# Attention in 64x64 tiles of TensorE, and router logits summed per head from the product that turns the outputs back

## The chip, the cores and the metric

The kernel runs on one NeuronCore of a Trainium2 chip. Its engines work side by side: TensorE (PE in the rows; PEld are its weight loads) multiplies matrices into PSUM, VectorE (DVE) and ScalarE (ACT) work element by element, GpSimd (POOL) does small work and indirect DMA, SyncE (SP) issues DMA. The metric is the time on the device in microseconds (us), the median of several runs; lower is better. The profile is of one execution.

## The reference

Block-sparse attention for 4 batches of 8 heads with 768 positions of 64 numbers, and then a mixture of 8 experts, of which a router with cosine similarity picks one for each of the 3072 tokens.

```python
# attention; mask[i, j] is set where the blocks of 32 positions of i and j are neighbours, one of
# them is the first or the last, or j's block is one of three drawn for i's
scores = np.where(mask, scale * np.matmul(q, k.transpose(0, 1, 3, 2)), -1000000000.0)
attn = np.exp(scores - np.max(scores, axis=-1, keepdims=True))
attn = attn / (np.sum(attn, axis=-1, keepdims=True) + 1e-09)
x = np.matmul(attn, v)                       # then (B, H, S, D) -> (B*S, H*D): 3072 x 512
...
xn = x / (np.linalg.norm(x, axis=-1, keepdims=True) + 1e-6)
en = expert_emb / (np.linalg.norm(expert_emb, axis=-1, keepdims=True) + 1e-6)
logits = xn @ en.T / tau
expert_idx = np.argmax(logits, axis=1)       # probs: the softmax of the logits
gate_w = probs[np.arange(N), expert_idx]
for e in range(E):
    mask = expert_idx == e
    out[mask] = gate_w[mask, None] * (np.maximum(x[mask] @ w1[e], 0.0) @ w2[e])
```

## The kernel before

Everything is float32 but the mask, which is bfloat16. There are two parts, one behind the other.

**Attention** (`attention_fast`). Work goes by pairs of heads, 16 of them, and in each pair by two halves of 384 queries. A half has six units, one for each 128 keys, so there are 192 units. `load_pair` brings a pair's keys, queries and values two pairs ahead. `turn_fast` turns keys and queries with TensorE, in four parts per pair (three 128x128 transposes each, copied out by VectorE for keys and by ScalarE for queries). `score_fast` makes a unit's scores for both heads: a mask product (24 rows of block numbers, line 272) opens each head's sum in PSUM, the product of keys and queries (64 rows, 128 columns of weights, line 275) closes it, and ScalarE takes the exponent (line 278) into SBUF, tile `e`. `attend_fast` multiplies `e` by the values: 128 rows and 64 columns of weights for each head (line 295), summed over the six units in PSUM tile `av`; VectorE sums `e` itself over the units into `esum` (lines 291 and 293). Behind the sixth unit ScalarE copies `av` to `at` (line 299). A float32 product of this kernel is two passes of TensorE, each with its weight load; so line 275 has 768 passes for 384 products.

`settle` ends a half, one unit later than its last: three transposes turn `at` back (line 313), six products with a column of ones make the sums over keys from `esum` (line 317, twelve passes of one column), and VectorE writes the outputs divided by these sums into `x` (line 323), one tile for a batch.

`route` follows each batch (four times): ScalarE squares `x` in six pieces (line 353) for the norms, POOL takes the root (line 354), TensorE transposes `x` in 24 blocks (line 363), VectorE copies them out (line 365), and 24 products in 48 passes of 8 columns (line 368) make the logits `lg` against the experts' normed vectors `en`. VectorE then finds the largest logit's place as a one-hot tile `oh` (line 385). Two small products (`rk`, lines 401 and 402) give each token its rank within its expert, of which the second waits for POOL's running counts `seen` (line 399).

`dispatch` then sorts the tokens into tiles of 128 of one expert (VectorE, and 24 products `slot_ps`).

**Experts.** For each of 27 such tiles weights and tokens are fetched by DMA, tokens transposed (`xg_ps`), multiplied by w1 (line 510) and w2 (line 518) and scattered to the output.

What sets the order: each engine has one queue in program order. The loop of `attention_fast` (line 545) names score products one unit ahead of the attention products, the turns in between, and settle and route behind the attention product of a half's second unit; the framework places the instructions of `route` among those of the following units by its own estimates. PSUM tiles come from pools: scores and router transposes from `big` (two buffers of two banks), `av` from `acc` (two buffers of one bank), everything small from `small` (two of one bank).

## Time and profile before

| | us |
|---|---|
| median of three runs | 1002.25 |
| lowest and highest run | 997.63, 1003.86 |
| the profiled execution, its run | 999.39 |
| the profiled execution, its span | 997.6 |
| mean granted TensorE clock | 0.947 |

Times in rows count from the span's start. A row of the timeline has a start, a length, the engine, the line, the operation, the tiles written and read with their shapes, the count of merged instructions and, in brackets, how long the engine sat idle before it and what ended that. A TensorE instruction's length contains its way through the array, so lengths of neighbours overlap, and the distance of starts is what one costs. The granted clock is a share of 2.4 GHz: 1.00 and 0.50 are the two levels.

### The profile page before, as it was taken

Reading aid. Unit: us, or ns where it says so; the run is one execution under the profiler, and the core shown is the slowest. Engines: PE = TensorE matmul, PEld = TensorE weight load, DVE = VectorE, ACT = ScalarE, POOL = GpSimd, SP = SyncE. Lnnn points to the kernel's source line nnn. Section 1 sums busy time; section 2 is a strip of 40 time slices with the busy share of each in tenths; the row PEclk is TensorE's granted clock in tenths of the full one; section 3 lists DMA queues with packets and bytes.
Section 4 is the critical chain, followed back from the end, with each engine's and each line's share of the span. In section 5 each row is a group of like instructions: output and inputs, shape, how many; then the busy total and the mean of one; then the engine's idle time right before and its main releaser. Section 6 shows DMA issues by size and latency. Waiting matters only on the chain.

```text
span 997.6 us, 12554 instructions
## 1 busy us (share of the span) xinstructions
PE 942.3 (94%) x5230; PEld 542.6 (54%) x5230; DVE 298.0 (30%) x513; ACT 218.0 (22%) x340; POOL 73.1 (7%) x105
## 2 busy tenths in 40 slices
PE   5999999999999999999998489999999999999984
PEld 2344354344454434634446466766776776776662
DVE  2444443444434444334444511111111111111110
ACT  2434432433423444233342000000000000000000
POOL 1000000000010000100001100110110111111010
PEclk9999996999979999789996589999999999999997
DMA  7111112111221111020001299989889998998872
GB/s 174 30 34 49 48 32 80 48 44 37 48 79 33 48 49 32 17 79 1 1 1 42 102 400 407 401 311 342 306 314 329 311 326 316 330 321 314 289 280 77
DMA packets 105243, 161.69 MB, mean 162 GB/s; under 512 B 52620, under 2 KB 56716, under 8 KB 104662
## 3 DMA queue, kind: packets, MB, share of 16 engines
q1 hardware_dynamic: 100694, 146.84, 43.3%
q0 software_dynamic: 4480, 13.91, 3.5%
q8 instruction: 45, 0.74, 0.3%
q14 instruction: 24, 0.20, 0.1%
HBM read 148.14 MB, written 13.38 MB: 162 GB/s over the span
## 4 chain that ended last, share of the span: by engine, by line
PE 89%; issue 5%; DVE 2%; DMA 1%; SPq 1%; ACT 0%; POOL 0%; POOLq 0%; ACTq 0%
PE sc L275 18%; PE hp L510 18%; PE yp L518 17%; PE av L295 16%; PE sc L272 5%; PE back L317 4%; PE turn L257 3%; PE lg L368 3%; PE back L313 2%; PE xg_ps L501 1%; PE slot_ps L462 1%; PE xt_ps L363 1%; DMA out_dram<-y,slot 1%; SPq L173 1%; DVE xt L365 0%
## 5 line engine op out<-in xcount | busy, mean ns | idle before, releaser
L278 ACT ACTIVATE e<-sc 128x768 f32<-128x768 f32 x192 | 155.6, 810 | 287.3 <-PE sc L275 287.3
L510 PEld LDWEIGHTS hp<-xgt,w 128*128 128x128 f32 x1728 | 199.5, 192 | 25.4 <-issue 11.0
L510 PE MATMUL hp<-xgt,w 128*128 128x128 f32 x1728 | 204.2, 277 | 9.1 <-ACT h L513 4.9
L275 PE MATMUL sc<-qt,kt 64*128 64x384 f32 x768 | 192.4, 556 | 0.0
L518 PE MATMUL yp<-w,h 128*128 128x512 f32 x432 | 189.9, 592 | 0.0
L295 PE MATMUL av<-e,vld 128*64 128x384 f32 x768 | 173.1, 523 | 0.0
L293 DVE TENSOR_TENSOR esum<-esum,e 128x768 f32<-128x768 f32 x128 | 122.3, 956 | 105.9 <-ACT e L278 105.9
L518 PEld LDWEIGHTS yp<-w,h 128*128 128x128 f32 x432 | 80.0, 190 | 90.4 <-issue 90.4
L513 ACT ACTIVATE h<-hp 128x512 f32<-128x512 f32 x27 | 16.1, 597 | 412.7 <-PE hp L510 383.7
L295 PEld LDWEIGHTS av<-e,vld 128*64 128x64 f32 x768 | 39.2, 137 | 81.9 <-issue 63.4
L275 PEld LDWEIGHTS sc<-qt,kt 64*128 64x128 f32 x768 | 62.6, 191 | 35.9 <-issue 35.8
L272 PEld LDWEIGHTS <-kmask 24*128 24x128 bf16 x384 | 18.2, 91 | 102.3 <-issue 101.8
L520 DVE TENSOR_SCALAR y<-yp,xg 128x512 f32<-128x512 f32 x27 | 20.3, 750 | 158.6 <-PE yp L518 158.6
L514 DVE TENSOR_SCALAR h<-hp 128x512 f32<-128x512 f32 x27 | 18.7, 691 | 160.9 <-PE hp L510 160.9
L272 PE MATMUL sc<-qmask,kmask 24*128 24x384 bf16 x384 | 66.5, 340 | 0.0
L291 DVE TENSOR_TENSOR esum<-e 128x768 f32<-128x768 f32 x32 | 30.7, 958 | 110.6 <-ACT e L278 110.6
L521 POOL DMA_INDIRECT out_dram<-y,slot x27 | 27.5, 1017 | 352.9 <-DVE y L520 338.5
L317 PEld LDWEIGHTS back<-ones,esum 128*128 128x128 f32 x384 | 45.4, 192 | 0.0
L317 PE MATMUL back<-ones,esum 128*128 128x1 f32 x384 | 44.7, 243 | 0.0
L354 POOL TENSOR_TENSOR nrm<-nrm,half 128x6 f32<-128x6 f32 x4 | 5.3, 1330 | 485.3 <-ACT sq L353 485.3
L368 PEld LDWEIGHTS lg<-en,xt 128*128 128x128 f32 x192 | 29.4, 242 | 6.3 <-DVE xt L365 4.6
L486 POOL DMA_INDIRECT xg<-x_dram,slot x29 | 29.9, 1032 | 29.2 <-DVE slot L464 20.6
(124 smaller groups left out, 392.8 us busy)
## 6 DMA issues: line engine op xcount, KB each, us to landing
w<-in_moe_w_dram SPq DMA_DIRECT2D x58, 2048.0 KB, 9.4
x_dram<-x SPq DMA_DIRECT2D x4, 1539.0 KB, 6.1
kld<-in_k_dram SPq DMA_DIRECT2D x32, 192.0 KB, 3.0
qld<-in_q_dram SPq DMA_DIRECT2D x32, 192.0 KB, 3.2
vld<-in_v_dram SPq DMA_DIRECT2D x16, 384.0 KB, 3.2
xg<-x_dram,slot POOLq DMA_INDIRECT x29, 7.4
out_dram<-y,slot POOLq DMA_INDIRECT x27, 7.4
x_dram<-zero SPq DMA_DIRECT2D x1, 2.0 KB
```

The source lines that it names most:

```text
L257: nc.tensor.transpose(ps[:, c * P:(c + 1) * P], src[:, lo + c].rearrange("p h d -> p (h d)"), k.ident)
L272: nc.tensor.matmul(ps[:, h, 0:HALF], lhsT=k.kmask[32 * h:32 * h + NB, keys], rhs=k.qmask[32 * h:32 * h + NB, queries], start=True, stop=False)
L275: nc.tensor.matmul(ps[:, h, 0:HALF], lhsT=kt[D * h:D * (h + 1), keys], rhs=qt[D * h:D * (h + 1), queries], start=False, stop=True)
L278: nc.scalar.activation(e, ps[:, :, 0:HALF], ACT.Exp)
L291: nc.vector.tensor_tensor(out=k.esum, in0=k.first, in1=e, op=ALU.add)
L293: nc.vector.tensor_tensor(out=k.esum, in0=k.esum, in1=e, op=ALU.add)
L295: nc.tensor.matmul(k.av[D * h:D * (h + 1), 0:HALF], lhsT=v[:, h, kc, :], rhs=e[:, h, :], start=(kc == 0), stop=(kc == NC - 1))
L317: nc.tensor.matmul(ps[:, i:i + 1], lhsT=esum[:, h, t * P:(t + 1) * P], rhs=k.ones[:, 0:1], start=True, stop=True)
L368: nc.tensor.matmul(lg[:, c, :], lhsT=xt[:, (c - c2) * ND + d, :], rhs=k.en[:, d, :], start=(d == 0), stop=(d == ND - 1))
L486: nc.gpsimd.indirect_dma_start(out=x[:, :], out_offset=None, in_=k.x_dram[:, :], in_offset=bass.IndirectOffsetOnAxis(ap=k.slot[:, t:t + 1] ...
L510: nc.tensor.matmul(hp[:, f, :], lhsT=w1[:, d, f * P:(f + 1) * P], rhs=xt[:, d, :], start=(d == 0), stop=(d == ND - 1))
L518: nc.tensor.matmul(yp, lhsT=h[:, f, :], rhs=w2[:, f, :], start=(f == 0), stop=(f == NF - 1))
```

## The change

It has six parts.

1. Masks, scores and attention products are cut into quarters: 64 rows (a head, or half of a unit's keys) by 64 columns. The mask's two tiles are widened from 24 to 64 rows of zeros for this. A unit has four mask products, four score products and four attention products where it had two of each; the sizes of `sc`, `e` and `esum` stay.
2. The attention products of the two halves of keys are summed apart: `av` has two banks, `acc` has one buffer in place of two, and behind the sixth unit ScalarE copies one bank (`part`) and VectorE adds the other to it (`at`).
3. `settle` turns back with a real product: its right side `back` has, for each of the two heads, a unit matrix of 64 columns and the 8 columns of `en` that belong to that head, 144 columns together. So partial logits per head come out beside the outputs; VectorE divides these too and keeps them in `part` for the batch.
4. `route` adds up the eight heads' partial logits on VectorE (`reduce_sum`); its transposes, their copies and its logit products are left out. They remain for the exact path, which runs only where a sum over keys is out of bounds.
5. The loop names scores two units ahead, settle and route first in a unit, then the attention product, a turn (at other units than before), and the scores.
6. Setup fills the mask tiles and `back`.

```diff
         for h in range(2):
-            nc.vector.tensor_copy(out=k.kmask[32 * h:32 * h + NB, :], in_=krow)
-            nc.scalar.copy(out=k.qmask[32 * h:32 * h + NB, :], in_=qr[0:NB, 0:S])
+            nc.vector.tensor_copy(out=k.kmask[D * h:D * h + NB, :], in_=krow)
+            nc.scalar.copy(out=k.qmask[D * h:D * h + NB, :], in_=qr[0:NB, 0:S])
...
+    k.back = k.const.tile([P, NPAIR, 2, D + E], F32, name="back")
+    nc.gpsimd.memset(k.back, 0.0)
+    for h in range(2):
+        rows = slice(D * h, D * (h + 1))
+        nc.vector.tensor_copy(out=k.back[rows, :, h, 0:D],
+                              in_=k.ident[rows, rows].unsqueeze(1).broadcast_to([D, NPAIR, D]))
+        nc.vector.tensor_copy(out=k.back[rows, :, h, D:D + E], in_=k.en[rows])
...
-    keys, queries = slice(kc * P, (kc + 1) * P), slice(qh * HALF, (qh + 1) * HALF)
-    for h in range(2):
-        nc.tensor.matmul(ps[:, h, 0:HALF], lhsT=k.kmask[32 * h:32 * h + NB, keys],
-                         rhs=k.qmask[32 * h:32 * h + NB, queries], start=True, stop=False)
-    for h in range(2):
-        nc.tensor.matmul(ps[:, h, 0:HALF], lhsT=kt[D * h:D * (h + 1), keys], rhs=qt[D * h:D * (h + 1), queries],
-                         start=False, stop=True)
+    queries = slice(qh * HALF, (qh + 1) * HALF)
+    quarters = [(h, r, slice(kc * P + D * r, kc * P + D * (r + 1))) for r in range(2) for h in range(2)]
+    for rows, cols, first in ((k.kmask, k.qmask, True), (kt, qt, False)):
+        for h, r, keys in quarters:
+            nc.tensor.matmul(ps[D * r:D * (r + 1), h, 0:HALF], lhsT=rows[D * h:D * (h + 1), keys],
+                             rhs=cols[D * h:D * (h + 1), queries], start=first, stop=not first)
...
-        k.av = k.acc.tile([P, 512], F32, name="av", tag="av")
+        k.av = k.acc.tile([P, 2, 512], F32, name="av", tag="av")
...
-    for h in range(2):
-        nc.tensor.matmul(k.av[D * h:D * (h + 1), 0:HALF], lhsT=v[:, h, kc, :], rhs=e[:, h, :],
-                         start=(kc == 0), stop=(kc == NC - 1))
+    for r in range(2):
+        for h in range(2):
+            nc.tensor.matmul(k.av[D * h:D * (h + 1), r, 0:HALF], lhsT=v[D * r:D * (r + 1), h, kc, :],
+                             rhs=e[D * r:D * (r + 1), h, :], start=(kc == 0), stop=(kc == NC - 1))
     if kc == NC - 1:
+        part = k.sp.tile([P, HALF], F32, name="part", tag="part")
+        nc.scalar.copy(out=part, in_=k.av[:, 1, 0:HALF])
         at = k.sp.tile([P, HALF], F32, name="at", tag="at")
-        nc.scalar.copy(out=at, in_=k.av[:, 0:HALF])
+        nc.vector.tensor_tensor(out=at, in0=k.av[:, 0, 0:HALF], in1=part, op=ALU.add)
...
     for t in range(NQ):
-        nc.tensor.transpose(ps[:, t * P:(t + 1) * P], at[:, t * P:(t + 1) * P], k.ident)
+        nc.tensor.matmul(ps[:, t * 2 * W:(t + 1) * 2 * W], lhsT=at[:, t * P:(t + 1) * P],
+                         rhs=k.back[:, j].rearrange("p h w -> p (h w)"), start=True, stop=True)
...
+    nc.vector.tensor_tensor(out=k.part[b][:, chunks, 2 * j:2 * j + 2, :], in0=rows[:, :, :, D:W],
+                            in1=inv.unsqueeze(3).broadcast_to([P, NQ, 2, E]), op=ALU.mult)
...
+    lg = logits(k, x) if k.exact else l
+    if not k.exact:
+        nc.vector.reduce_sum(out=l, in_=k.part[b].rearrange("p c h e -> p c e h"), axis=AX.X)
...
-    n.big, n.acc = pool("big_f", 2, space=PSUM), pool("acc", 2, space=PSUM)
+    n.big, n.acc = pool("big_f", 2, space=PSUM), pool("acc", 1, space=PSUM)
...
     score_fast(n, 0)
+    score_fast(n, 1)
     for u in range(units):
         g = u // per
         if u % per == 0 and g + 2 < pairs:
             load_pair(n, g + 2)
-        if u + 1 < units:
-            score_fast(n, u + 1)
-        if u % per in (2, 4, 8, 10) and g + 1 < pairs:
-            turn_fast(n, g + 1, (2, 4, 8, 10).index(u % per))
-        attend_fast(n, u)
         if u % NC == 1 and u > NC:
             settle(n, u // NC - 1)
             if (u - 1) % (per * NPAIR) == 0:
                 route(n, (u - 1) // (per * NPAIR) - 1)
+        attend_fast(n, u)
+        if u % per in (2, 3, 5, 8) and g + 1 < pairs:
+            turn_fast(n, g + 1, (2, 3, 5, 8).index(u % per))
+        if u + 2 < units:
+            score_fast(n, u + 2)
```

Three places of the order show how it stands in the queues. In these rows `x4` counts products that follow each other, and the shape is that of what is written.

TensorE before, around a settle: the end of one unit's scores, its attention products, the settle (`back`), and the next unit with a turn.

```order
L275 MATMUL sc<-qt,kt 128x384 x2
L295 MATMUL av<-e,vld 64x384 x2
L313 MATMUL back<-ident,at 128x128 x3
L317 MATMUL back<-ones,esum 128x1 x6
L272 LDWEIGHTS kmask
L272 MATMUL sc<-qmask,kmask 128x384
L272 LDWEIGHTS kmask
L272 MATMUL sc<-qmask,kmask 128x384
L275 MATMUL sc<-qt,kt 128x384 x2
L257 MATMUL turn<-ident,qld 128x128 x3
L295 MATMUL av<-e,vld 64x384 x2
```

TensorE with the change, around a settle: from the end of a unit's scores to the next unit's first score product.

```order
L283 MATMUL sc<-qt,kt 64x384 x4
L327 MATMUL back<-back,at 128x144 x3
L332 MATMUL back<-ones,esum 128x1 x6
L304 MATMUL av<-e,vld 64x384 x4
L283 LDWEIGHTS kmask
L283 MATMUL sc<-qmask,kmask 64x384
L283 LDWEIGHTS kmask
L283 MATMUL sc<-qmask,kmask 64x384
L283 LDWEIGHTS kmask
L283 MATMUL sc<-qmask,kmask 64x384
L283 LDWEIGHTS kmask
L283 MATMUL sc<-qmask,kmask 64x384
```

Products are twice as many and half as tall, the settle stands ahead of the attention products, and its transposes have become products of 144 columns.

TensorE before, at the first router pass, behind the settle of the batch's last half:

```order
L313 MATMUL back<-ident,at 128x128 x3
L317 MATMUL back<-ones,esum 128x1 x6
L363 MATMUL xt_ps<-ident,x 128x128 x15
L295 MATMUL av<-e,vld 64x384
L368 MATMUL lg<-en,xt 128x8 x8
L295 MATMUL av<-e,vld 64x384
L363 MATMUL xt_ps<-ident,x 128x128 x9
L368 MATMUL lg<-en,xt 128x8 x8
```

TensorE with the change, at the first router pass; ahead of these rows and behind the settle stand the attention products of two units and the scores of one.

```order
L283 MATMUL sc<-qt,kt 64x384 x4
L304 MATMUL av<-e,vld 64x384
L425 MATMUL rk<-oh,before 128x48
L266 MATMUL turn<-ident,kld 128x128 x2
L426 MATMUL rk<-seen,ones 128x48
L266 MATMUL turn<-ident,kld 128x128
L304 MATMUL av<-e,vld 64x384 x3
L283 LDWEIGHTS kmask
L283 MATMUL sc<-qmask,kmask 64x384
L266 MATMUL turn<-ident,kld 128x128 x3
```

Transposes and logits are gone; the rank products stand two units behind the settle, in the middle of an attention product's quarters and a turn.

ScalarE with the change, at the first router pass (`e<-sc` are exponents of units, `part<-av` the new copy of an accumulator's bank, `sq` the squares):

```order
L286 ACTIVATE e<-sc 128x768 x3
L308 COPY part<-av 128x384
L286 ACTIVATE e<-sc 128x768 x2
L387 ACTIVATE sq,nrm<-x 128x512 x3
L286 ACTIVATE e<-sc 128x768
L412 ACTIVATE l<-l 128x48
L286 ACTIVATE e<-sc 128x768 x3
```

ScalarE before, at the same place:

```order
L299 COPY at<-av 128x384
L278 ACTIVATE e<-sc 128x768 x2
L353 ACTIVATE sq,nrm<-x 128x512 x3
L278 ACTIVATE e<-sc 128x768
L388 ACTIVATE l<-l 128x48
L278 ACTIVATE e<-sc 128x768 x3
L299 COPY at<-av 128x384
```

Here little moved: the last three squares stand behind the second exponent of the half, as they did.

## Rows read from the trace of the kernel before

**Rows 1.** The page, parts 1 and 4: busy engines, and the chain by line.

```profile
PE 942.3 (94%) x5230; PEld 542.6 (54%) x5230; DVE 298.0 (30%) x513; ACT 218.0 (22%) x340; POOL 73.1 (7%) x105
PE sc L275 18%; PE hp L510 18%; PE yp L518 17%; PE av L295 16%; PE sc L272 5%; PE back L317 4%; PE turn L257 3%; PE lg L368 3%; PE back L313 2%; PE xg_ps L501 1%; PE slot_ps L462 1%; PE xt_ps L363 1%; DMA out_dram<-y,slot 1%; SPq L173 1%; DVE xt L365 0%
```

**Rows 2.** Stretches: length, busy PE, PEld, DVE, ACT, POOL; clock, DMA share, GB/s.

```profile
25.00:60.00 35.00, 35.00 (x201) 14.13 (x199) 16.22 (x23) 13.86 (x19) 0.00 (x0) 1.00 0.14 35
...
600.00:700.00 100.00, 99.41 (x563) 71.48 (x562) 14.46 (x21) 3.58 (x6) 12.41 (x13) 1.00 0.96 362
```

**Rows 3.** Timeline of one unit on TensorE, and the next unit's first product.

```profile
204.14 0.33 PE L272 MATMUL sc<-qmask,kmask 24*128 24x384 bf16 x2
204.41 0.59 PE L275 MATMUL sc<-qt,kt 64*128 64x384 f32 x2
204.83 0.49 PE L275 MATMUL sc<-qt,kt 64*128 64x384 f32 x2
205.25 0.87 PE L295 MATMUL av<-e,vld 128*64 128x384 f32 x4
...
206.05 0.34 PE L272 MATMUL sc<-qmask,kmask 24*128 24x384 bf16 x2
```

**Rows 4.** Timeline: a settle, a turn behind it, and an expert tile's second product.

```profile
200.04 0.55 PE L313 MATMUL back<-ident,at 128*128 128x128 f32 x3
200.32 1.42 PEld L317 LDWEIGHTS back<-ones,esum 128*128 128x128 f32 x12
201.76 0.34 PE L272 MATMUL sc<-qmask,kmask 24*128 24x384 bf16 x2
202.87 0.55 PE L257 MATMUL turn<-ident,qld 128*128 128x128 f32 x3
203.34 0.87 PE L295 MATMUL av<-e,vld 128*64 128x384 f32 x4
...
588.13 7.03 PE L518 MATMUL yp<-w,h 128*128 128x512 f32 x16
```

**Rows 5.** Timeline: starts of the settles around the first router pass, and of the last.

```profile
137.96 0.55 PE L313 MATMUL back<-ident,at 128*128 128x128 f32 x3
...
171.80 0.55 PE L313 MATMUL back<-ident,at 128*128 128x128 f32 x3
...
185.92 0.55 PE L313 MATMUL back<-ident,at 128*128 128x128 f32 x3
...
528.64 0.55 PE L313 MATMUL back<-ident,at 128*128 128x128 f32 x3
```

**Rows 6.** Stretches as in rows 2, in the first router pass and at attention's end.

```profile
150.40:167.40 17.00, 17.00 (x50) 7.38 (x51) 5.86 (x17) 2.84 (x5) 1.90 (x6) 0.50 0.32 116
...
532.60:580.40 47.80, 28.49 (x130) 26.98 (x130) 20.67 (x71) 2.19 (x7) 6.78 (x11) 0.50 0.35 131
```

**Rows 7.** Groups by line: count | busy us, mean ns | idle before, releaser.

```profile
L278 ACT ACTIVATE e<-sc 128x768 f32<-128x768 f32 x192 | 155.6, 810 | 287.3 <-PE sc L275 287.3
L299 ACT COPY at<-av 128x384 f32<-128x384 f32 x32 | 15.3, 480 | 1.3 <-PE av L295 1.3
L353 ACT ACTIVATE sq<-x 128x512 f32<-128x512 f32 x24 | 14.9, 622 | 27.9 <-DVE x L323 27.9
...
L323 DVE TENSOR_TENSOR x<-back,inv 128x384 f32<-128x384 f32 x32 | 17.8, 557 | 1.0
...
L354 POOL TENSOR_TENSOR nrm<-nrm,half 128x6 f32<-128x6 f32 x4 | 5.3, 1330 | 485.3 <-ACT sq L353 485.3
```

**Rows 8.** Timeline: the last one-hot, and the first expert tile's transposes.

```profile
544.94 0.21 DVE L385 TENSOR_TENSOR oh<-pick,mx 128x48 f32<-128x48 f32 x1
...
575.23 4.39 PE L501 MATMUL xg_ps<-ident,xg 128*128 128x128 f32 x16 [8.86 <-issue]
```

**Rows 9.** Timeline: a half's last attention products, and ScalarE's copy of their sum.

```profile
209.55 0.87 PE L295 MATMUL av<-e,vld 128*64 128x384 f32 x4
...
210.46 0.48 ACT L299 COPY at<-av 128x384 f32<-128x384 f32 x1
```

More of the change, by code (lines that the diff above doesn't have):

```diff
@@ L310, in settle @@
         k.x[b] = k.xp.tile([P, NC, XW], F32, name="x", tag="x")
+        k.part[b] = k.xp.tile([P, NC, H, E], F32, name="part", tag="part")
     ps = k.small.tile([P, 512], F32, name="back", tag="small")
+    W = D + E
+    rows = ps[:, 0:NQ * 2 * W].rearrange("p (t h w) -> p t h w", t=NQ, h=2)
     for t in range(NQ):
-        nc.tensor.transpose(ps[:, t * P:(t + 1) * P], at[:, t * P:(t + 1) * P], k.ident)
+        nc.tensor.matmul(ps[:, t * 2 * W:(t + 1) * 2 * W], lhsT=at[:, t * P:(t + 1) * P],
+                         rhs=k.back[:, j].rearrange("p h w -> p (h w)"), start=True, stop=True)
+    i = NQ * 2 * W
     for t in range(NQ):
         for h in range(2):
-            i = HALF + 2 * t + h
-            nc.tensor.matmul(ps[:, i:i + 1], lhsT=esum[:, h, t * P:(t + 1) * P], rhs=k.ones[:, 0:1],
-                             start=True, stop=True)
+            nc.tensor.matmul(ps[:, i + 2 * t + h:i + 2 * t + h + 1], lhsT=esum[:, h, t * P:(t + 1) * P],
+                             rhs=k.ones[:, 0:1], start=True, stop=True)
     den = k.dens[:, w, :]
-    nc.vector.tensor_scalar(out=den, in0=ps[:, HALF:HALF + 2 * NQ], scalar1=1e-9, scalar2=None, op0=ALU.add)
+    nc.vector.tensor_scalar(out=den, in0=ps[:, i:i + 2 * NQ], scalar1=1e-9, scalar2=None, op0=ALU.add)
     inv = k.sp.tile([P, NQ, 2], F32, name="inv", tag="inv")
     nc.vector.reciprocal(out=inv.rearrange("p t h -> p (t h)"), in_=den)
+    chunks = slice(qh * NQ, (qh + 1) * NQ)
     nc.vector.tensor_tensor(
-        out=k.x[b][:, qh * NQ:(qh + 1) * NQ, j * P:(j + 1) * P].rearrange("p t (h d) -> p t h d", h=2),
-        in0=ps[:, 0:HALF].rearrange("p (t h d) -> p t h d", t=NQ, h=2),
-        in1=inv.unsqueeze(3).broadcast_to([P, NQ, 2, D]), op=ALU.mult)
+        out=k.x[b][:, chunks, j * P:(j + 1) * P].rearrange("p t (h d) -> p t h d", h=2),
+        in0=rows[:, :, :, 0:D], in1=inv.unsqueeze(3).broadcast_to([P, NQ, 2, D]), op=ALU.mult)
+    nc.vector.tensor_tensor(out=k.part[b][:, chunks, 2 * j:2 * j + 2, :], in0=rows[:, :, :, D:W],
+                            in1=inv.unsqueeze(3).broadcast_to([P, NQ, 2, E]), op=ALU.mult)
 def count_good(k):
@@ L344, in count_good, with logits @@
     nc.vector.tensor_copy(out=k.good, in_=ps[:, 0:1])
-def route(k, b):
-    nc, p, x = k.nc, k.rp, k.x[b]
-    nrm = p.tile([P, NC], F32, name="nrm")
-    for c in range(NC):
-        sq = p.tile([P, DM], F32, name="sq")
-        nc.scalar.activation(sq, x[:, c, 0:DM], ACT.Square, accum_out=nrm[:, c:c + 1])
-    nc.gpsimd.tensor_tensor(out=nrm, in0=nrm, in1=k.half, op=ALU.pow)
-    nc.vector.tensor_scalar(out=nrm, in0=nrm, scalar1=1e-6, scalar2=None, op0=ALU.add)
-    nc.vector.reciprocal(out=nrm, in_=nrm)
+def logits(k, x):
+    nc, p = k.nc, k.rp
     lg = k.small.tile([P, NC, E], F32, name="lg", tag="small")
@@ L369, in route @@
                                  start=(d == 0), stop=(d == ND - 1))
+    return lg
+def route(k, b):
+    nc, p, x = k.nc, k.rp, k.x[b]
+    nrm = p.tile([P, NC], F32, name="nrm")
+    for c in range(NC):
+        sq = p.tile([P, DM], F32, name="sq")
+        nc.scalar.activation(sq, x[:, c, 0:DM], ACT.Square, accum_out=nrm[:, c:c + 1])
+    nc.gpsimd.tensor_tensor(out=nrm, in0=nrm, in1=k.half, op=ALU.pow)
+    nc.vector.tensor_scalar(out=nrm, in0=nrm, scalar1=1e-6, scalar2=None, op0=ALU.add)
+    nc.vector.reciprocal(out=nrm, in_=nrm)
     def wide(t):
@@ L628 @@
     n.loaded, n.vs, n.es, n.ets, n.sums, n.x, n.fetched = {}, {}, {}, {}, {}, {}, {}
-    n.turned, n.done = {}, {}
+    n.turned, n.done, n.part = {}, {}, {}
     n.exact = False
```

2 lines of the change are left out of this document (added).

## The prediction

> **What bounds the kernel now.** I read the page's first and fourth part first: TensorE is busy 94% of the span, and the chain that ended last is TensorE work, with the score, attention and expert products as its largest shares [rows 1]. Then the stretches: in the attention part TensorE is busy all the time while VectorE and ScalarE are busy under half of it, and in the expert part TensorE is busy as well, with the DMA engines at 0.96 [rows 2]. So attention ends with TensorE, and the expert part, which the change leaves alone, is a constant of about 422 us (first expert instruction at 575.2, end of the span at 997.6 [rows 8, 1]).
>
> Next one unit (128 keys, 384 queries, two heads) in the timeline. Mask products start at 204.14, score products at 204.41, their second passes at 204.83, attention products at 205.25, the next unit's mask at 206.05 [rows 3]: 0.27 + 0.84 + 0.80 = 1.91 us. What of this is columns? The expert product of 512 columns repeats every (7.03 - 0.59) / 15 = 0.429 us [rows 4], that is 0.84 ns a column, so a float32 pass of 384 columns needs 0.322 us. Both heads' passes run side by side (two starts at 204.41, two at 204.83), so scores need 0.64 of their 0.84 us and attention 0.64 of its 0.80. A mask product lasts 0.33 us, a second score pass 0.49 [rows 3]; the 0.16 between them is half a pass, so I take 0.16 as its columns. Columns make 1.45 us of the unit, and 0.46 us is gap. The gaps stand where the tile shape changes: 24x128 rows by columns for the mask, 64x128 for scores, 128x64 for attention. Within one shape there is none: three transposes of 128 columns and the twelve 1-column passes behind them start 0.11 us apart without a break [rows 4].
>
> Last the rhythm. A half (six units, one settle, two turns) takes 14.12 us, read from the distance 171.80 to 185.92; where a router pass lies in between it takes 171.80 - 137.96 = 33.84 us [rows 5]. So a router pass costs 19.7 us there, on a path that TensorE sets, and much of it runs at granted clock 0.50, the 1.2 GHz level [rows 6].
>
> **The change, part by part.**
>
> *Quarters.* Mask, scores and attention all become 64x64 tiles, so nothing changes shape inside a unit. The columns stay: four tiles at once carry what two carried, 0.16 + 0.64 + 0.64 = 1.45 us. Below that the unit can't go. From above: 20 pairs of weight load and pass per unit in place of 10, and the quickest long run of pairs in the trace is one per 0.112 us ((1.42 - 0.19) / 11 in the settle [rows 4]), which would make 2.24 us. That run is bound by loading 128 columns, though, and the unit's weights are 64 columns wide and go to four tiles; pairs on two tiles start within hundredths of each other now [rows 3]. So I take it nearer the lower end: 1.50 us, with 0.05 us for tiles that start late. 0.1 us more or less in a unit is 19 us over 192 units.
>
> *Settle.* Three transposes become three real products with 144 columns and two passes each: 6 x 0.121 = 0.73 us in place of 3 x 0.11, so +0.40. It now is one of the few places where the shape changes; entering from the quarters 0.10, leaving 0.05. The 1.72 us from its start to the next mask [rows 4] become about 2.4 with these. *Turns.* 202.87 to 203.34 is 0.47 us now [rows 4]; with a shape change on either side 0.62, twice a half.
>
> *One accumulator.* The pool for the attention sum has one buffer of two banks, where there were two of one. The first attention product of a half must wait for ScalarE's copy and VectorE's add of the half before. With T as the end of the last attention columns: the exponent of the next unit lasts 0.81 us and began 0.64 - 0.22 before T, so it ends at T + 0.39 (0.22 is the lag from columns to ScalarE: the last pass starts at 209.92 by the pattern of rows 3, ends 0.32 later, the copy starts at 210.46 [rows 9]). Copy 0.48, add as long as the like operation on 384 elements, 0.56 [rows 7]: T + 1.43, with handovers T + 1.5. TensorE has 0.80 us of scores to do meanwhile, and in every second half a turn of 0.62. It waits 0.7 or 0.1 us, 0.45 in the mean with the weights loaded late.
>
> A half: 6 x 1.50 + 2.4 + 2 x 0.62 + 0.45 = 13.1 in place of 14.12. Times 32: **-33 us**. VectorE gets the add, and a small product (48 elements) per half, ScalarE no more than before; both stay under 7.1 us of 13.1 per half and cover these.
>
> *Router.* 24 transposes, 48 logit passes and three copies go. What is left is a chain: settle 2.3, VectorE's four operations to x and the partial logits 1.2, three squares 3 x 0.62 + 0.1, POOL's root 1.33 [rows 7], then nine small VectorE operations near 0.24 with one 0.96 us sum in between, so that the one-hot is there some 9.9 us after the settle's start. In the order the rank product stands behind two units and a piece, at about 6.3 us: TensorE waits 3.5 us, then 1.3 us for POOL's running counts; and an exponent queued behind the three squares costs it 1 us ahead of that. With the rank products 7 us. TensorE is idle for several us, so I expect the clock to fall for a while too (now 17 us at 0.50 [rows 6]): a 60% chance of some 7 us lost to it, 4 in the mean. 11 us in place of 19.2 (the mean of three), three times: **-25 us**. Bounds: 6 (chain all hidden but for the two waits, full clock) and 19 (clock as now).
>
> *Tail.* From the last settle (528.64) to the one-hot's end (544.94 + 0.21) are 16.5 us now [rows 5, 8], most of them at clock 0.50 [rows 6]. The chain above, without the 0.96 us sum in it, is 9.0 us with no transposes and logits in the way: **-7.5 us**. Dispatch behind it is VectorE's and stays.
>
> *Setup.* Three memsets on POOL and four copies on VectorE; the block numbers' DMA ends later than these, but two copies of 64x4x8 stand before the first turned keys: +0.4.
>
> Sum: -33 - 25 - 7.5 + 0.4 = -65. The profiled run took 999.4 (span 997.6), so 934; its median of three was 1002.25, 2.9 above. I say **936 us**.
>
> **A rule against it.** The rows show that the heads' passes overtake: the program names one head's product, then the other's, each with two passes, yet two starts lie at 204.41 and two at 204.83 [rows 3], and scores take 0.84 us with their gaps. The Trainium skill, page "TensorE: Matmul & The Clock Gate", Part 3 on packing small matmuls, says that matmuls start and end strictly in program order. By that rule two heads would need three passes in a row, 0.97 us without gaps; the trace has less, so it does not agree. By the rule four quarters would need five passes, 1.61 us a stage, and a unit 3.4 us.
>
> **Rivals.**
> *A, forecast*: four tiles run at once and without gaps, 58%; 905 to 965 us of its own.
> *B, the tiles are filled too slowly*: four quarters need twice the pairs, and a tile whose work stands far back in the queue starts late. At 0.112 us a pair the unit is 2.24 us: 936 + 0.74 x 192 = 1078 us. It decides from 1.85 us a unit on, where all the gain is used up (65 / 192 = 0.34). For it: no row has 20 pairs in 1.5 us. Against: the starts within hundredths. 16%, about half of it between 1.65 and 1.85.
> *C, only two of four quarters run at once* (two that share rows, or share columns, exclude each other): 0.32 + 1.29 + 1.29 = 2.9 us, 936 + 1.4 x 192 = 1205 us. Against it: the two score tiles share their columns and the two attention tiles their rows, and both pairs run together now [rows 3]. Program order as the wall would be 936 + 1.9 x 192 = 1300. Together 7%.
> *D, the gaps stay*, since they come from changing the operand or the bank and not the shape: the unit is 1.9 again, the settle dearer, the router still cheaper: 936 + 0.4 x 192 = 1013. Against: transposes and 1-column passes change operand without a gap [rows 4]. 8%.
> *E, more than forecast*: unit 1.45 (-10), the router's waits mostly hidden and full clock, 5 us each time (-18), most waits for the accumulator gone (-9): 899 or below. 11%.
>
> **How the numbers follow.** The likeliest case gives 936. Below 900 I leave some 8%, above 1010 C and the upper end of B, 12%: range 900 to 1010. One per cent, 10 us, is about what a measurement of this kernel can tell from no change. Faster by over 1%: A, E and the lower half of B, 0.76. Within 1%: the middle of B and most of D, 0.09. Slower: C and the rest, 0.15.
>
> **What would show it.** Right: score and attention passes of a unit start as two groups of four, 0.32 us apart, with no 0.1 us step from mask to scores to attention; unit 1.5 us; halves of 13.1; routed halves near 24; one-hot 9 us behind the last settle; expert part 422 us. Wrong: quarters' starts spread over half a pass or more (B), groups of two (C), a step of 0.1 us at each stage (D), an attention product waiting on VectorE's add for over 1 us each half, or a clock of 0.50 outside the router passes.

## The result and the profile after

The changed kernel takes **914.0 us** (median of four runs, 913.36 to 914.92), the kernel before 1003.06 beside it (997.63 to 1004.47). The ratio is 0.912 with a 95% interval of 0.909 to 0.916: faster by 9%. The forecast was 936 with a range of 900 to 1010. The profiled execution has a span of 912.3 us, where that of before had 997.6, and a mean granted clock of 0.959.

The page of the changed kernel, part 1 and the shares by engine of part 4, to be laid beside [rows 1]; the last line is the kernel before's chain by engine:

```profile
PE 831.0 (91%) x6958; PEld 528.8 (58%) x6958; DVE 312.5 (34%) x573; ACT 216.2 (24%) x340; POOL 74.9 (8%) x108
PE 81%; issue 6%; DVE 5%; ACT 4%; DMA 2%; POOL 2%; POOLq 0%; DVEq 0%; SPq 0%; ACTq 0%
...
PE 89%; issue 5%; DVE 2%; DMA 1%; SPq 1%; ACT 0%; POOL 0%; POOLq 0%; ACTq 0%
```

TensorE has 1728 more passes and yet 111 us less busy time, and is still the engine on which most of the chain runs. VectorE got 14.5 us more work, and of the chain VectorE and ScalarE now have 5% and 4% where they had 2% and 0%; where TensorE waits for them is shown further on.

One unit on TensorE, timeline as in [rows 3] (start, length, engine, line, operation, count):

```profile
203.00 0.33 PE L283 MATMUL sc<-qmask,kmask 64*64 64x384 bf16 x4
203.17 0.81 PE L283 MATMUL sc<-qt,kt 64*64 64x384 f32 x8
203.81 0.81 PE L304 MATMUL av<-e,vld 64*64 64x384 f32 x8
204.46 0.33 PE L283 MATMUL sc<-qmask,kmask 64*64 64x384 bf16 x4
```

Mask to mask is 1.46 us where it was 1.91: 0.17 for the mask, 0.64 for the scores, 0.65 for the attention products. That is the 1.45 us that the columns take by the prediction's estimate, and no gap. A shorter stretch shows the first four score passes by themselves, and the second row gives the length of a pass (least, median and most, ns):

```profile
203.17 0.49 PE L283 MATMUL sc<-qt,kt 64*64 64x384 f32 x4
...
L283 PE MATMUL sc<-qt,kt x8: 482/482/483, 203.2 to 203.5; 64*64 64x384 f32 x8
```

Four passes of 0.48 us each lie in 0.49 us, so their starts are within 0.01 us; all eight lie in 0.81, so the second four start 0.32 us behind the first.

A settle, the counterpart of [rows 4], and the starts of settles around the first router pass and behind it, the counterparts of [rows 5]:

```profile
196.63 1.00 PE L327 MATMUL back<-back,at 128*128 128x144 f32 x6
197.47 1.40 PE L332 MATMUL back<-ones,esum 128*128 128x1 f32 x12
198.79 0.88 PE L304 MATMUL av<-e,vld 64*64 64x384 f32 x8
199.49 0.34 PE L283 MATMUL sc<-qmask,kmask 64*64 64x384 bf16 x4
...
124.59 1.00 PE L327 MATMUL back<-back,at 128*128 128x144 f32 x6
...
146.13 1.00 PE L327 MATMUL back<-back,at 128*128 128x144 f32 x6
...
158.46 1.00 PE L327 MATMUL back<-back,at 128*128 128x144 f32 x6
...
183.70 1.00 PE L327 MATMUL back<-back,at 128*128 128x144 f32 x6
```

A half takes 12.33 us (146.13 to 158.46) or 12.93 (183.70 to 196.63), in turn: 12.62 in the mean where it was 14.12. With a router pass in it, it takes 21.54 (124.59 to 146.13); the two later passes have 21.34 and 21.26. So a pass costs 8.8 us over the mean half, where it cost 19.2.

The first router pass on all engines, with waits in brackets:

```profile
129.73 0.79 ACT L286 ACTIVATE e<-sc 128x768 f32<-128x768 f32 x1
130.57 0.85 PE L304 MATMUL av<-e,vld 64*64 64x384 f32 x2 [0.68 <-ACT e L286]
133.88 0.21 DVE L409 TENSOR_TENSOR oh<-pick,mx 128x48 f32<-128x48 f32 x1
134.15 0.66 PE L425 MATMUL rk<-oh,before 128*128 128x48 f32 x2 [2.72 <-DVE oh L409]
136.28 0.66 PE L426 MATMUL rk<-seen,ones 128*128 128x48 f32 x2 [1.02 <-POOL seen L423]
```

TensorE waits for an exponent that stands behind the squares, then for the one-hot, then for POOL's counts: 4.42 us. And the clock falls, as the stretches show (length; busy PE, PEld, DVE, ACT, POOL with counts; clock; DMA share; GB/s): this pass, attention's end, and a stretch between passes.

```profile
134.00:141.00 7.00, 5.83 (x29) 3.34 (x33) 2.73 (x8) 0.35 (x1) 1.94 (x6) 0.51 0.55 227
451.60:496.00 44.40, 19.41 (x86) 17.93 (x86) 20.43 (x75) 2.19 (x7) 6.75 (x11) 0.50 0.43 161
200.00:215.00 15.00, 14.55 (x176) 7.62 (x172) 7.67 (x12) 6.60 (x10) 0.00 (x0) 1.00 0.22 55
```

At each of the three passes some 6.8 us run at 0.50, the 1.2 GHz level, where [rows 6] has 17 us at the first pass before.

The end of attention: the last settle, the last one-hot, the first transposes of the experts; of before [rows 5, 8] have 528.64, 544.94 and 575.23.

```profile
449.44 1.00 PE L327 MATMUL back<-back,at 128*128 128x144 f32 x6 [1.19 <-DVE at L310]
...
458.34 0.21 DVE L409 TENSOR_TENSOR oh<-pick,mx 128x48 f32<-128x48 f32 x1
...
488.42 3.22 PE L525 MATMUL xg_ps<-ident,xg 128*128 128x128 f32 x12 [8.65 <-issue]
```

From the last settle to the one-hot's end are 9.1 us where there were 16.5, and to the experts 39.0 where there were 46.6.

So the 85.3 us between the spans lie here (first settle of before at 39.12, of after at 36.52):

| stretch | before | after | difference |
|---|---|---|---|
| up to the first settle | 39.1 | 36.5 | -2.6 |
| first to last settle | 489.5 | 412.9 | -76.6 |
| last settle to the experts | 46.6 | 39.0 | -7.6 |
| experts | 422.4 | 423.9 | +1.5 |

In the second row, 31 halves with 1.50 us less each are -46.5 and three router passes with 10.4 less each are -31: together -77.7. (The first settle stands ahead of an attention product now, where it stood behind one, so some 0.65 us of the gain went from the second row to the first.)

### The profile page after: what moved, and what is told of

Its sections match the earlier page's. It is cut to its first block, busy times and chain, and to the rows that moved or that the text cites. A ratio compares the mean times of both kernels' runs of the same rounds, so it can differ in the third digit from the quotient of the medians.

```text
span 912.3 us, 16075 instructions
## 1 busy us (share of the span) xinstructions
PE 831.0 (91%) x6958; PEld 528.8 (58%) x6958; DVE 312.5 (34%) x573; ACT 216.2 (24%) x340; POOL 74.9 (8%) x108
## 4 chain that ended last, share of the span: by engine, by line
PE 81%; issue 6%; DVE 5%; ACT 4%; DMA 2%; POOL 2%; POOLq 0%; DVEq 0%; SPq 0%; ACTq 0%
PE hp L534 19%; PE yp L542 18%; PE sc L283 16%; PE av L304 13%; PE back L332 4%; PE turn L266 4%; PE back L327 3%; ACT e L286 1%; PE slot_ps L486 1%; DVE at L310 1%; ACT sq L387 1%; PE xg_ps L525 1%; ACT part L308 1%; DMA xg<-x_dram,slot 1%; DMA out_dram<-y,slot 1%
## 5 line engine op out<-in xcount | busy, mean ns | idle before, releaser
L304 PE MATMUL av<-e,vld 64*64 64x384 f32 x1536 | 167.4, 497 | 9.6 <-DVE at L310 7.2
L283 PE MATMUL sc<-qt,kt 64*64 64x384 f32 x1536 | 161.9, 490 | 0.0
L304 PEld LDWEIGHTS av<-e,vld 64*64 64x64 f32 x1536 | 53.8, 134 | 75.8 <-issue 27.7
L283 PEld LDWEIGHTS sc<-qt,kt 64*64 64x64 f32 x1536 | 58.5, 135 | 29.3 <-issue 26.0
L544 DVE TENSOR_SCALAR y<-yp,xg 128x512 f32<-128x512 f32 x27 | 20.3, 751 | 158.9 <-PE yp L542 158.9
L283 PE MATMUL sc<-qmask,kmask 64*64 64x384 bf16 x768 | 70.4, 335 | 0.0
L283 PEld LDWEIGHTS <-kmask 64*64 64x64 bf16 x768 | 24.5, 107 | 34.1 <-issue 33.6
L327 PEld LDWEIGHTS back<-back,at 128*128 128x128 f32 x192 | 25.2, 189 | 20.4 <-issue 18.6
L327 PE MATMUL back<-back,at 128*128 128x144 f32 x192 | 32.1, 303 | 1.2 <-DVE at L310 1.2
```

What stands on the lines that cost most here:

```text
L283: nc.tensor.matmul(ps[D * r:D * (r + 1), h, 0:HALF], lhsT=rows[D * h:D * (h + 1), keys], rhs=cols[D * h:D * (h + 1), queries], start=first ...
L304: nc.tensor.matmul(k.av[D * h:D * (h + 1), r, 0:HALF], lhsT=v[D * r:D * (r + 1), h, kc, :], rhs=e[D * r:D * (r + 1), h, :], start=(kc == 0 ...
L327: nc.tensor.matmul(ps[:, t * 2 * W:(t + 1) * 2 * W], lhsT=at[:, t * P:(t + 1) * P], rhs=k.back[:, j].rearrange("p h w -> p (h w)"), start= ...
L544: nc.vector.tensor_scalar(out=y, in0=yp, scalar1=x[:, DM:XW], scalar2=None, op0=ALU.mult)
```

## Experiments

The theory (S) says: the gaps in a unit stand where the tile shape changes, and four quarters of one shape run at once. Its rivals: the gaps come from how wide the weights are (W), or the gain comes from the new order of the loop, which names scores two units ahead (O). For the router the theory is that TensorE waits in the pass and that the low clock follows these waits.

### One shape less, and nothing else

`mask64` is the kernel before with the mask tiles widened to 64 rows of zeros, so that mask and scores have the same shape. All products stay as wide and as many as they were.

```diff
+        nc.gpsimd.memset(k.kmask, 0.0)
+        nc.gpsimd.memset(k.qmask, 0.0)
...
-            nc.vector.tensor_copy(out=k.kmask[32 * h:32 * h + NB, :], in_=krow)
-            nc.scalar.copy(out=k.qmask[32 * h:32 * h + NB, :], in_=qr[0:NB, 0:S])
+            nc.vector.tensor_copy(out=k.kmask[D * h:D * h + NB, :], in_=krow)
+            nc.scalar.copy(out=k.qmask[D * h:D * h + NB, :], in_=qr[0:NB, 0:S])
...
-        nc.tensor.matmul(ps[:, h, 0:HALF], lhsT=k.kmask[32 * h:32 * h + NB, keys],
-                         rhs=k.qmask[32 * h:32 * h + NB, queries], start=True, stop=False)
+        nc.tensor.matmul(ps[:, h, 0:HALF], lhsT=k.kmask[D * h:D * (h + 1), keys],
+                         rhs=k.qmask[D * h:D * (h + 1), queries], start=True, stop=False)
```

> The kernel before with one edit: the mask tiles are widened from 24 to 64 rows with zeros, so mask and score products have one tile shape (64 rows by 128 columns) and the attention products another. Theory S (the gaps inside a unit stand where the tile shape changes): the step from mask to scores falls from 0.27 us to the 0.16 us of the mask's columns, 0.1 us in each of 192 units, so 1003 - 20 = 983 us; the other two steps stay. Theory W (the gaps are weight loads that nothing covers, and shrink only because quarters have half the columns): the mask's and the scores' weights are as wide as before, so 1003 us. Theory O (the gain came from naming scores two units ahead): 1003 us.

Measured: **952.5 us**, ratio 0.952 (0.951 to 0.954). The timeline of a unit, with the load of the scores' weights:

```profile
200.07 0.34 PE L274 MATMUL sc<-qmask,kmask 64*128 64x384 bf16 x2
200.07 0.36 PEld L277 LDWEIGHTS sc<-qt,kt 64*128 64x128 f32 x4
200.24 0.81 PE L277 MATMUL sc<-qt,kt 64*128 64x384 f32 x4
200.98 0.87 PE L297 MATMUL av<-e,vld 128*64 128x384 f32 x4
201.78 0.34 PE L274 MATMUL sc<-qmask,kmask 64*128 64x384 bf16 x2
```

The unit falls from 1.91 to 1.71 us: the mask takes 0.17 where it took 0.27, and the scores 0.74 where they took 0.84. More zeros in the weights make the kernel faster by 47 us. The width of the weights, the products and the order are as before, so W and O can't explain it. The size was missed by half, though: a shape change less saves 0.2 us and not 0.1. The second tenth stands in the scores, and the weight loads go with it. In this kernel the loads of the scores' weights begin at 200.07, with the mask's product. In the kernel before they begin only with the first score product (the mask's product starts at 204.14 [rows 3]):

```profile
204.41 0.30 PEld L275 LDWEIGHTS sc<-qt,kt 64*128 64x128 f32 x4 [0.17 <-issue]
```

So behind this change of shape two delays show: the score products start 0.27 us behind the mask's, whose columns take 0.16, and their weights, which otherwise are loaded beside the columns ahead, are loaded only then (the first passes last 0.59 us, the second 0.49 [rows 3]).

The 0.2 us a unit make 38 of the 47 us. Most of the rest lies in the three halves with a router pass: they take 28.9 us each, where they took 33.85, 32.3 and 33.8, and so shrink by 13.2 us together, of which the units' share is 3.6. There the stretch at clock 0.50 is 10.2 us long in place of 17.1, 13.7 and 17.1; why it is shorter was not tried. The first of the three in `mask64` (columns as in the stretches above):

```profile
140.70:151.00 10.30, 10.30 (x36) 5.51 (x35) 4.35 (x15) 1.75 (x3) 1.89 (x6) 0.51 0.18 77
```

### The quarters alone

`quarters_only` is the kernel before with the change's quarters, wider mask and two banks of one accumulator; settle, router and loop stay.

```diff
-    for h in range(2):
-        nc.tensor.matmul(k.av[D * h:D * (h + 1), 0:HALF], lhsT=v[:, h, kc, :], rhs=e[:, h, :],
-                         start=(kc == 0), stop=(kc == NC - 1))
+    for r in range(2):
+        for h in range(2):
+            nc.tensor.matmul(k.av[D * h:D * (h + 1), r, 0:HALF], lhsT=v[D * r:D * (r + 1), h, kc, :],
+                             rhs=e[D * r:D * (r + 1), h, :], start=(kc == 0), stop=(kc == NC - 1))
```

> The kernel before with the quarters alone: 64x64 tiles for mask, scores and attention, the two-bank accumulator with one buffer and the copy and add behind it; the loop (scores one unit ahead), the settle with transposes and the router with its own logits are those of before. Theory S: a unit falls from 1.91 to 1.45 us, 192 x 0.46 = 88 us; against it 0.15 us more at each settle and turn (3 x 32, 14 us) and a wait for the one accumulator of 0.3 to 0.6 us a half (10 to 20 us): 1003 - 88 + 14 + 15 = 944 us, units of 1.45 us in the trace. Theory O: with scores one unit ahead the units stay well above 1.45 us, attention products wait for exponents, 980 us or more.

Measured: **944.8 us**, ratio 0.945 (0.943 to 0.946). The unit is 1.45 us with scores only one unit ahead:

```profile
202.01 0.82 PE L276 MATMUL sc<-qt,kt 64*64 64x384 f32 x8
202.66 0.82 PE L297 MATMUL av<-e,vld 64*64 64x384 f32 x8
203.30 0.34 PE L276 MATMUL sc<-qmask,kmask 64*64 64x384 bf16 x4
203.47 0.82 PE L276 MATMUL sc<-qt,kt 64*64 64x384 f32 x8
204.73 0.88 PE L297 MATMUL av<-e,vld 64*64 64x384 f32 x8 [0.44 <-DVE at L303]
```

Scores to scores is 1.46 (202.01 to 203.47). The last row is the price of the single accumulator: 1.26 us from scores to attention products where a unit without the wait has 0.65. O falls.

### The change with the old shapes

`old_shapes` is the changed kernel with the mask, score and attention products of before and two accumulators; settle, router and loop are the new ones.

```diff
-    n.big, n.acc = pool("big_f", 2, space=PSUM), pool("acc", 1, space=PSUM)
+    n.big, n.acc = pool("big_f", 2, space=PSUM), pool("acc", 2, space=PSUM)
```

> The changed kernel with mask, score and attention products in the shapes of before (24x128, 64x128, 128x64; one bank and two buffers for the accumulator, ScalarE's copy alone); the new loop, the settle with the 144-column product and the router without its own logits stay. Theory S: units are 1.91 us again, 192 x 0.46 = 88 us more; 14 us less at settles and turns and about 10 us less for the accumulator: 914 + 88 - 24 = 978 us. Theory O: the loop keeps the gain, 930 us or less.

Measured: **983.5 us**, ratio 0.983 (0.982 to 0.985), and units of 1.91:

```profile
204.89 0.34 PE L279 MATMUL sc<-qmask,kmask 24*128 24x384 bf16 x2
205.16 0.92 PE L282 MATMUL sc<-qt,kt 64*128 64x384 f32 x4
206.00 0.87 PE L302 MATMUL av<-e,vld 128*64 128x384 f32 x4
206.80 0.34 PE L279 MATMUL sc<-qmask,kmask 24*128 24x384 bf16 x2
```

Loop, settle and router without the quarters are worth 16 us (5 less than theory S had said; why was not tried). The quarters on top of them bring 983 to 914.

### The change with the old router

`old_router` is the changed kernel with the transposes of before in `settle` and with the logits of `route` from its own transposes.

```diff
-        nc.tensor.matmul(ps[:, t * 2 * W:(t + 1) * 2 * W], lhsT=at[:, t * P:(t + 1) * P],
-                         rhs=k.back[:, j].rearrange("p h w -> p (h w)"), start=True, stop=True)
+        nc.tensor.transpose(ps[:, t * P:(t + 1) * P], at[:, t * P:(t + 1) * P], k.ident)
...
-    lg = logits(k, x) if k.exact else l
-    if not k.exact:
-        nc.vector.reduce_sum(out=l, in_=k.part[b].rearrange("p c h e -> p c e h"), axis=AX.X)
+    lg = logits(k, x)
```

> The changed kernel with the settle's transposes and the router's own transposes and logits of before; the quarters and the new loop stay. From the traces of both kernels: a router pass costs 8.8 us instead of 19.2 with the change (three times 10.4, 31 us), the stretch from the last settle to the first expert tile 39.0 instead of 46.6 (7.6 us), and the settle's real products cost 0.4 us more a half (13 us). So undoing the router's part alone gives 914 + 31 + 8 - 13 = 940 us, and stretches at granted clock 0.50 of some 15 us at each router pass come back. If the router's part were worth nothing net (the settle eats it up): 914 us.

Measured: **940.9 us**, ratio 0.942 (0.939 to 0.945). Its halves are 11.87 and 12.47 us, 0.45 less than with the real products in the settle; a routed half takes 32.0, 30.4 and 30.4, so a pass costs about 19 as it did before. Between first and last settle old_router has 433.3 us (36.24 to 469.55), the changed kernel 412.9. The new way to logits thus pays 0.45 x 31 = 14 us in the settles and gets back 33 in the three passes and the halves ahead of them (12.88 there in place of 11.87), and 5 more up to the experts (513.74 - 469.55 = 44.2 in place of 39.0). Against `quarters_only`, which has the same router but the old loop, the halves are 12.17 us in the mean in place of 12.50, and first to last settle 433.3 in place of 441.7. So the loop's new order shows in the trace; but 3 us of this are lost again behind the last settle, the medians lie 4 us apart, and the intervals of the ratio overlap, so what it is worth in the kernel's time can't be told closer than that.

### The mask's old shape in the changed kernel

`mask_old_shape` is the changed kernel with the two mask products of before, 24 rows by 128 columns. If shape changes cost, this brings back two per unit.

```diff
-    for rows, cols, first in ((k.kmask, k.qmask, True), (kt, qt, False)):
-        for h, r, keys in quarters:
-            nc.tensor.matmul(ps[D * r:D * (r + 1), h, 0:HALF], lhsT=rows[D * h:D * (h + 1), keys],
-                             rhs=cols[D * h:D * (h + 1), queries], start=first, stop=not first)
+    for h in range(2):
+        nc.tensor.matmul(ps[:, h, 0:HALF], lhsT=k.kmask[32 * h:32 * h + NB, kc * P:(kc + 1) * P],
+                         rhs=k.qmask[32 * h:32 * h + NB, queries], start=True, stop=False)
+    for h, r, keys in quarters:
+        nc.tensor.matmul(ps[D * r:D * (r + 1), h, 0:HALF], lhsT=kt[D * h:D * (h + 1), keys],
+                         rhs=qt[D * h:D * (h + 1), queries], start=False, stop=True)
```

> The changed kernel with the mask products alone in the shape of before (24 rows by 128 columns, two of them); scores and attention stay in quarters. A unit then has two places where the tile shape changes, into the mask and out of it, where the changed kernel has none, the kernel before has three (unit 1.91 us) and the one with widened masks has two (unit 1.71 us). If the cost goes with the number of these places, as 0.46 us for three and 0.26 for two say, a unit takes 1.45 + 0.26 = 1.71 us: 914 + 192 x 0.26 = 964 us. If the mask's step alone were the dear one (it cost 0.20 us before), 0.20: 952 us. If the number of products sets it and not the shape, nothing or a gain: 914 us or less.

Measured: **955.5 us**, ratio 0.954 (0.951 to 0.957). The timeline, with a turn behind the unit:

```profile
206.07 0.33 PE L280 MATMUL sc<-qmask,kmask 24*128 24x384 bf16 x2
206.34 0.88 PE L283 MATMUL sc<-qt,kt 64*64 64x384 f32 x8
207.03 0.82 PE L304 MATMUL av<-e,vld 64*64 64x384 f32 x8
207.79 0.55 PE L264 MATMUL turn<-ident,kld 128*128 128x128 f32 x3
```

Mask 0.27, scores 0.69, attention 0.76: 1.71 to 1.72 us again, with half as many mask products as the changed kernel. So two changes cost 0.26 us a unit here and in `mask64`, three cost 0.46, none costs nothing. Per half the loss is 1.17 us and not 6 x 0.26 = 1.56: a turn or settle that stands beside the mask has its change already paid, and in the halves without a turn at their end the wait for the accumulator is shorter (1.05 us from scores to attention products, where the changed kernel has 1.27). So the run lies between the two expected figures. The Trainium skill says on its page "TensorEngine Tiling (Array Packing)", section "Tiling Modes", that switching the tiling mode drains the engine. The unit's times in `before`, `mask64` and `mask_old_shape` agree with it, and add a price and the later weight load in the rows beside `mask64`: what was expected of a drain alone was 0.1 us, and 0.2 came.

### The router's rank products later

`rank_late` is the changed kernel with the two rank products and what follows them in a function of their own, called five units behind their batch's `route`.

```diff
+    if k.exact or b == B - 1:
+        rank(k, b)
+
+def rank(k, b):
     rk = k.small.tile([P, NC, E], F32, name="rk", tag="small")
...
+        if u % (per * NPAIR) == 6 and u > per * NPAIR:
+            rank(n, u // (per * NPAIR) - 1)
```

> The changed kernel with the two rank products of a router pass (and the VectorE work on them) named five units later, where the one-hot and the running counts are long there; they were the ones that TensorE waited for (2.7 and 1.0 us at the first pass). Theory: these waits make the router pass dear, and the granted clock of 0.50 for 6.8 us behind them follows from TensorE standing idle. Then the router pass falls from 8.8 us to about 1.5: 3.7 us of waits, 3.4 us from the clock, three times, 21 us: 893 us, with the clock at 1.00 through the passes. Rival: the clock falls all the same, since the 1-column products of the settle and the wait for an exponent behind the squares are what it follows: 11 us, 903 us, and the stretches at 0.50 stay. Second rival: the wait only moves to another product: 914 us.

Measured: **898.5 us**, ratio 0.897 (0.895 to 0.900). Intervals with a pass take 16.0, 17.7 and 17.6 us where they took 21.5, 21.3 and 21.3, the stretch at 0.50 is gone at the first pass and 3.4 us long at the others, and the rank products wait for nothing. The time lies between the theory's 893 and the rival's 903. One wait stays; the rows show it at the first pass, then at the second, with the stretch at 0.50 behind it:

```profile
133.08 0.24 ACT L412 ACTIVATE l<-l 128x48 f32<-128x48 f32 x1 [3.23 <-DVE pick L406]
...
134.08 0.88 PE L304 MATMUL av<-e,vld 64*64 64x384 f32 x8 [1.88 <-ACT e L286]
...
238.13 1.17 PE L304 MATMUL av<-e,vld 64*64 64x384 f32 x8 [1.86 <-ACT e L286]
...
238.60:242.00 3.40, 3.40 (x28) 1.10 (x20) 1.80 (x3) 0.98 (x2) 2.10 (x5) 0.50 0.90 351
```

ScalarE stood 3.23 us at the exponent of the logits, which waits for VectorE, while a unit's exponent stood behind it. ScalarE had this wait in the changed kernel too (2.88 us), but there TensorE's wait for the one-hot covered it. So a pass still costs 3.1 to 4.8 us over the half in whose place it stands (12.92); counted so, it costs 8.3 to 8.6 in the changed kernel. The clock is only half explained: TensorE waits the same 1.9 us at all three passes, and yet it falls at two of them and not at the first. To place that exponent later as well was not tried.

### The turn under the accumulator's wait

`turn11` is the changed kernel with the fourth turn of a pair at the last unit of a pair's second half, so that both kinds of halves have a turn beside the copy and the add of the accumulator.

```diff
-        if u % per in (2, 3, 5, 8) and g + 1 < pairs:
-            turn_fast(n, g + 1, (2, 3, 5, 8).index(u % per))
+        if u % per in (2, 3, 5, 11) and g + 1 < pairs:
+            turn_fast(n, g + 1, (2, 3, 5, 11).index(u % per))
```

> The changed kernel with the fourth turn of a pair named at unit 11 in place of 8, so that each half has a turn between its last attention product and the next half's first. Halves take 12.32 and 12.92 us in turn; the first kind holds one turn and waits 0.6 us for the accumulator (copy and add), the second holds three turns, one of them in that place, and does not wait. Theory: the turn fills the wait, 0.6 us in each of 16 pairs, 10 us: 904 us. Rival: the copy of the turned queries on ScalarE, or the add, comes later for it, and the wait stays: 914 us.

Measured: **907.4 us**, ratio 0.906 (0.903 to 0.909). The two kinds of halves in the changed kernel, the one without cover and the one with a turn, show what it moves:

```profile
206.07 0.81 PE L283 MATMUL sc<-qt,kt 64*64 64x384 f32 x8
207.34 0.88 PE L304 MATMUL av<-e,vld 64*64 64x384 f32 x8 [0.45 <-DVE at L310]
...
193.89 0.47 ACT L308 COPY part<-av 128x384 f32<-128x384 f32 x1
194.40 0.56 DVE L310 TENSOR_TENSOR at<-av,part 128x384 f32<-128x384 f32 x1 [0.52 <-ACT part L308]
195.06 0.83 PE L304 MATMUL av<-e,vld 64*64 64x384 f32 x8
```

Without cover scores to attention products is 1.27 us in place of 0.64, with a turn (193.75 to 194.22) the add has ended at 194.96 when the products come at 195.06. In `turn11` the first kind of half falls from 12.32 to 11.71 and the second stays at 12.93: the wait is gone. Only 6.8 us reach the span (905.5), though, where 16 x 0.61 = 9.8 were to be had: the half ahead of each router pass falls to 12.02 only, and the routed intervals are 21.67, 22.47 and 21.20 where they were 21.54, 21.34 and 21.26, the second with 10.2 us at 0.50 in place of 6.8. Part of the gain is given back where the router's waits stand next; why the half ahead of a pass keeps 0.3 us was not tried.

### Both

`both` is the changed kernel with the two edits above.

> Both edits at once: rank products five units later, and the fourth turn at unit 11. They touch different waits, so the theories add up: 914 - 21 - 10 = 883 us. If the clock falls all the same: 893 us.

Measured: **890.0 us**, ratio 0.890 (0.887 to 0.893), a span of 887.2: faster than either of the two kernels. Its halves are 11.71 and 12.93. The stretches of the first routed half and of attention's end:

```profile
122.25:138.26 16.01, 14.04 (x156) 7.28 (x152) 10.64 (x28) 7.49 (x15) 4.08 (x7) 1.00 0.40 122
426.90:471.00 44.10, 19.37 (x87) 17.91 (x87) 20.43 (x75) 2.19 (x7) 6.78 (x11) 0.50 0.42 158
```

The routed half has 16.0 us at clock 1.00 throughout; what a pass costs is 3.1 us over its own kind of half (12.93). At no pass does the clock fall any more. The time is 7 us above the sum of the theories (883): the exponent's wait of 1.9 us is left at each pass, and the turn brought 7 us and not 10. In `rank_late` and `both`, six passes without the waits for the rank products, the stretch of 6.8 us at 0.50 never comes: it is gone at four and 3.4 us long at two. That speaks for those waits as the cause of its length. It does not say when the clock falls at all, for the wait that is left is the same 1.9 us at all six. At attention's end, where TensorE is busy 19.4 of 44.1 us, it stays at 0.50.

## Why the prediction was right, and where its sizes were off

**The bound and the gaps** were right. TensorE set attention's time, the 0.46 us of gaps stood at changes of shape, and `mask64` and `mask_old_shape` show it with a change taken out and put back. The steps at each stage (rival D) are gone, the starts come in fours (against B and C). Of the signs of being wrong one is there by the letter, a clock of 0.50 outside the router passes at attention's end (451.6 to 496.0); but it stood there before as well [rows 6], so it says nothing against the forecast.

**The unit** was taken at 1.50 us with 0.05 for tiles that start late; nothing starts late, and it is 1.45 to 1.46. That is 0.27 us a half.

**The settle** was put at 2.4 us with its entry and exit. It is 196.63 to 198.79, 2.16, and 0.11 and 0.06 more in the neighbours (scores 195.87 to 196.63 in place of 0.65, attention products 0.70 in place of 0.64): 2.33. **The turn** was put at 0.62 and is 201.05 to 201.53 with 0.1 for what stands beside it: right.

**The single accumulator** was put at 0.7 or 0.1 us. It is 0.62 where no turn stands beside it and nothing where one does: the mean is 0.31 and not 0.45.

With these, a half is 6 x 1.455 + 2.33 + 0.62 + 0.62 = 12.3 or 6 x 1.455 + 2.33 + 3 x 0.62 = 12.9, and that is what the settles' distances show. The forecast 13.1 was high by 0.48: 0.27 from the unit, 0.07 from the settle, 0.14 from the accumulator. Over 32 halves this is 15 us. As a span the forecast was 933 (997.6 - 65), 20 above the measured 912.3.

**The router** was put at 11 us a pass and costs 8.8. The three waits were seen in their places: 3.5, 1.3 and 1 us forecast, 2.72, 1.02 and 0.68 measured, 1.4 less. The fall of the clock was given a chance of 60% and a price of 7 us, 4 in the mean. It came each time, but its price was mis-sized: the 6.8 us at half the clock contain the wait for the counts, and of the 5.8 us of work in them half is lost, 2.9 us. With two rank products at full clock, 0.5, these estimates make 7.8 of the 8.8; the last 1.0 was not followed up. Three passes with 2.2 us less each are 6.6 us.

**The tail** was put at 9.0 us to the one-hot and is 9.1; -7.5 forecast, -7.6 measured. **Setup**: the first attention products start their rhythm at the same time (24.80 before, 24.84 after, the mask behind them), so the +0.4 did not come. The expert part is 1.5 us longer, 0.4%; why was not tried. So 15 from the halves, 6.6 from the router and 0.4 from setup, less 1.5 in the experts, are 20.5 where 20.3 are to be explained. That it agrees so well is partly luck: attention's last two halves, which have no turns, gain 0.65 us together (22.41 to 21.76) and not 3.0, while those between gain 1.54 each and not 1.50, and the first settle comes 2.6 us earlier.

**The rule against it**, that products start and end strictly in program order (the Trainium skill, "TensorE: Matmul & The Clock Gate", Part 3), forecast a unit of 3.4 us. In the changed kernel each quarter's two passes stand together in the program, and yet the first passes of four quarters start within 0.01 us and the eight passes cost 0.64. The trace doesn't agree with it for products on different tiles.

Rival E named the three terms on which more could be had (unit, router's waits, accumulator), with 899 us as their sum. In the change itself the unit's came whole and the other two in part; `both`, where two of them were taken out, ends at 890.

## What to carry to other kernels

Look at the tile shapes that follow each other on TensorE, not only at how full each is: here a mask padded with zeros to its neighbour's shape was worth 47 us of 1000 by itself (38 in the units, most of the rest in the router passes), and quarters that carry the same columns brought the unit to its columns. Where a chain on other engines ends in a small product, name that product late enough that TensorE has full units to do meanwhile; here five units later made a half with a router pass 3.6 to 5.5 us shorter. A single accumulator was free here where a turn stood beside its copy and add, and cost 0.62 us a half where none did, so place such work there by hand, and look then at what the next wait is.

## What had not been expected of the hardware

- A change of tile shape cost 0.13 to 0.2 us at the 2.4 GHz level (0.26 us for two, 0.46 for three). In the kernel before, the first score weights behind it were not loaded beside the columns ahead; in `mask64`, without that change, they were, and 0.10 us went from the mask and 0.10 from the scores.
- 20 pairs of weight load and pass fitted in 1.45 us, one per 0.073 us, when they went to four tiles; the quickest run on one tile had one per 0.112 [rows 4].
- Passes of different tiles overtook in the queue: eight float32 passes that stand as four pairs in the program ran as two groups of four, 0.32 us apart.
- In the routed halves of the changed kernel the granted clock fell to 0.50 at the rank product, for which TensorE had waited 2.72 us (at the later two passes 0.3 and 0.5 us ahead of it, within a wait of 2.69), and stayed there for 6.8 us; in `both`, where TensorE's one long wait in the routed half was 1.89 us, it stayed at 1.00. A wait of that length does not decide it, though: in `rank_late` the clock fell for 3.4 us behind waits of 1.86 us at two passes and stayed at 1.00 behind one of 1.88 at the first.
